# A hand-written TensorE order for the transform of a spectral layer: one pattern per step, the halves of the first stage set apart

## Chip, cores and metric

One core of one Trainium2 chip. The metric is device time in microseconds (us); the kernel before has a median of 1771.21 us over 3 runs (1770.46 to 1773.0).

## What is computed

`x` is (8, 3136, 256) in float32. The reference takes a real FFT over the sequence, multiplies by a complex 256x256 matrix, adds a complex bias, shrinks real and imaginary parts towards zero, transforms back, and feeds the result to a feed-forward block with a 3-tap convolution and a gate:

```python
X = np.fft.rfft(x, axis=1)
Yr = Xr @ w_r - Xi @ w_i + b_r
Yi = Xr @ w_i + Xi @ w_r + b_i
Y = sign(Y) * maximum(abs(Y) - 0.01, 0)          # both parts
y = np.fft.irfft(Y, n=3136, axis=1)
h = maximum(y @ w_in, 0)                          # 256 -> 1024
c = conv_w[0] * h[t-1] + conv_w[1] * h[t] + conv_w[2] * h[t+1]
out = (h * sigmoid(c)) @ w_out                    # 1024 -> 256
```

## The kernel before

3136 is 56 times 56, so each transform is two stages of products with small tables. The work of the transform is cut into 56 items, 7 for each of the 8 batches. It runs as a loop over steps (L373); step `it` touches several items at once:

- `load_a2` (L268) asks for the second-stage input of item it+2 from the DRAM scratch `sc1`.
- `stage2` (L273): eight float32 products of 128 columns on TensorE (PE), L280. ScalarE (ACT) and VectorE (DVE) split the result into a high part `fh` (L284, L287) and a low part `fl` (L286, L288), for products in three pieces.
- `load_inv1` and `load_t2`, in the first seven steps only: pieces of the tables of the inverse and the forward transform. Each piece of the inverse table lands in `i_raw`, which has two buffers; ACT casts it (L140, tile `i_hi`) and DVE takes the difference (L141, `i_lo`).
- `mix` (L291): the complex matrix on item it-1, as three groups of twelve products of 256 columns (L304), in three PSUM tiles `ps_mx`. DVE adds bias and combines (L309, L313), ACT and DVE shrink (L318, L319), ACT casts to `sh` (L320), GpSimd makes `sl`.
- `stage3` (L324): twelve products on item it-3 (L331), whose copy `z1` goes to the scratch `sc2`.
- `stage1` (L239): the first stage of an item some ten places ahead. Two float32 products of 512 columns (L245), called halves below. Both write the one buffer of the PSUM pool `ps1`, so a half can't begin before ACT has copied the half before it into `a1` (L246). `a1` has two buffers; each whole `a1` goes to `sc1` by a DMA (L247), so the third item after the head can't be copied before the first one's store has landed. The loaded `xr` has three buffers.

The first stage of the first batch's seven items stands before the loop (`stage1_head`, L249). Two more items, 7 and 8, are called ahead of the loop (L358 to L360). Item 7's two halves, item 8's and then item 9's are the first halves that this text speaks of.

The order of the instructions on each engine is not the written one: the program is built with a scheduler that orders every engine by its own estimate of times (`schedule_with_timeline_sim`, L537). All DMAs are issued on SyncE's queue (SP), in order. After the transform come `stage4` (L416) and the feed-forward loop (`up`, `down`, L432 to L484).

Of the kernel before, what the change touches and what calls it, by code (L numbers as in the profile page):

```python
# [9 lines left out]
F32 = mybir.dt.float32  # L10
# [4 lines left out]
ALU = mybir.AluOpType  # L15
# [3 lines left out]
B, S, D, FF = 8, 3136, 256, 1024  # L19
# [3 lines left out]
SP = 64  # L23
H = 28
LAM = 0.01
UG = 4
NG = U // UG
JC = 4
# [68 lines left out]
def spectral_ffn_kernel(ctx: ExitStack, tc: tile.TileContext, x, w_r, w_i, b_r, b_i,  # L97
                        w_in, conv_w, w_out, fwd1, fwd2, inv1, inv2, out):
    nc = tc.nc
    K1, K2 = 2 * R, 2 * SP  # L100

    dram = ctx.enter_context(tc.tile_pool(name="dram", bufs=1, space=DRAM))
    sc1 = [dram.tile([K1, H, D], F32, name=f"sc1_{b}") for b in range(B)]
# [13 lines left out]
    with ExitStack() as ab:  # L117
# [15 lines left out]
        bias = cmx.tile([P, 2, UG // 2, D], F32, name="bias")  # L133
# [60 lines left out]
        def split_weight(dst, raw, n, name):  # L194

            top, rest = yield from from_bits(raw, n, name)
            h, l = dst
            nc.scalar.copy(h, top)
            yield nc.vector.tensor_tensor(top, top, h.bitcast(F32), op=ALU.subtract)
            yield nc.vector.tensor_tensor(l, top, rest, op=ALU.add)  # L200
# [6 lines left out]
        def later():  # L207
            nc.sync.dma_start(i2, inv2)
            bits = [load_bits(conv_w[k].rearrange("(f p) w -> p f w", p=P), NF, "cw") for k in range(2)]
            for k in range(3):  # L210
                top, rest = yield from from_bits(bits[k], NF, "cw")
                yield nc.vector.tensor_tensor(cw[:, k, :], top, rest, op=ALU.add)  # L212
                if k == 0:
                    bits.append(load_bits(conv_w[2].rearrange("(f p) w -> p f w", p=P), NF, "cw"))
            pieces = []
            for t in range(NT):
                for c in range(0, FF, WP):
                    pieces.append(([q[:, t, c:c + WP] for q in win], winv[:, t, c:c + WP, :], "win"))
            for f in range(0, NF, 2):
                pieces.append(([q[:, f:f + 2, :].rearrange("p a d -> p (a d)") for q in wout], woutv[:, f:f + 2, :, :], "wout"))  # L220
            asked = []
            for n in range(len(pieces) + 1):
                if n < len(pieces):
                    dst, src, nm = pieces[n]
                    asked.append((dst, load_bits(src, WP, nm), WP, nm))
                    yield None
                if n:
                    yield from split_weight(*asked.pop(0))

        def load_x(pool, b, jc, parts=1, **kw):  # L230

            xr = pool.tile([K1, JC, D], F32, name="xr", **kw)
            xv = x[b].rearrange("(n j) d -> n j d", j=H)[:, jc * JC:(jc + 1) * JC, :]
            w = JC // parts
            for k in range(0, JC, w):
                ld = nc.sync.dma_start(xr[:, k:k + w, :], xv[:, k:k + w, :])
            return xr, ld

        def stage1(b, jc):  # L239

            xr, _ = load_x(s1p, b, jc, bufs=XRB)
            a1 = s1p.tile([K1, JC, D], F32, name="a1", bufs=2)
            for j in range(0, JC, 2):
                ps = ps1.tile([K1, 2, D], F32, name="ps_s1")
                nc.tensor.matmul(ps, f1, xr[:, j:j + 2, :], start=True, stop=True)  # L245
                nc.scalar.copy(a1[:, j:j + 2, :], ps)  # L246
            return nc.sync.dma_start(sc1[b][:, jc * JC:(jc + 1) * JC, :], a1)  # L247

        def stage1_head(xs, b=0):  # L249

# [17 lines left out]
        def load_a2(b, g):  # L268
            a2 = a2p.tile([K1, UG, D], F32, name="a2")
            ld = nc.sync.dma_start(a2, sc1[b].rearrange("(u q) j d -> (q j) u d", q=4)[:, g * UG:(g + 1) * UG, :])  # L270
            return a2, ld
# [16 lines left out]
            nc.vector.tensor_tensor(fl[:, :, 2], d, fh[:, :, 2].bitcast(F32), op=ALU.subtract)  # L288
            return fh, fl

        def mix(xs):  # L291


            fh, fl = xs
            ps = [psm.tile([K2, UG // 2, D], F32, name=f"ps_mx{c}") for c in range(3)]
            for c in (2, 0, 1):
                q = (1, 2, 0)[c]
                for k in range(UG // 2):
                    mm = []
                    for t in range(NT):  # L300
                        a = [f[:, t, c, 2 * k:2 * k + 2, :] for f in (fh, fl)]
                        mm += [(a[0], wmix_hi[:, t, q, :]), (a[0], wmix_lo[:, t, q, :]), (a[1], wmix_hi[:, t, q, :])]
                    for n, (lt, rh) in enumerate(mm):
                        nc.tensor.matmul(ps[c][:, k, :], lt, rh, start=(n == 0), stop=(n == len(mm) - 1))  # L304
            p1 = wk.tile([K2, 2, UG // 2, D], F32, name="p1", bufs=1)
            v = wk.tile([K2, UG // 2, 2, D], F32, name="v")
            half = (slice(0, SP), slice(SP, K2))
            for c in range(2):
                nc.vector.tensor_tensor(p1[:, c], ps[2], bias[:, c], op=ALU.add)  # L309
            for c in range(2):  # L310
                for k in range(2):
                    src, dst = half[k], half[k if c == 0 else 1 - k]
                    nc.vector.tensor_tensor(v[dst, :, k, :], ps[c][src], p1[src, c], op=ALU.add)  # L313
            v = v.rearrange("p a b d -> p (a b) d")
            sh = wk.tile([K2, UG, D], F32R, name="sh")
            sl = wk.tile([K2, UG, D], F32R, name="sl", bufs=1)
            r = wk.tile([K2, UG, D], F32, name="r", bufs=1)
            nc.scalar.activation(r, v, AF.Relu, bias=mlam)  # L318
            thr = nc.vector.scalar_tensor_tensor(v, v, LAM, r, op0=ALU.add, op1=ALU.min)  # L319
            nc.scalar.copy(sh, v)  # L320
            SL_ENG.tensor_tensor(sl, v, sh.bitcast(F32), op=ALU.subtract)  # L321
            return sh, sl, thr

        def stage3(b, g, s):  # L324

            sh, sl, _ = s
            ps = psa.tile([K1, UG, D], F32, name="ps_s3")
            for k in range(UG):
                u = g * UG + k
                for n, (lt, rh) in enumerate(((i1_hi, sh), (i1_hi, sl), (i1_lo, sh))):  # L330
                    nc.tensor.matmul(ps[:, k, :], lt[:, u, :], rh[:, k, :], start=(n == 0), stop=(n == 2))  # L331
            z1 = io.tile([K1, UG, D], F32, name="z1", bufs=2)
            nc.scalar.copy(z1, ps)
            nc.sync.dma_start(sc2[b][:, g * UG:(g + 1) * UG, :], z1)

        nc.vector.memset(mlam, -LAM)
        nc.vector.memset(warm, 0.0)
        nc.scalar.activation(warm, warm, AF.Sigmoid)

        AHEAD = NG + 3  # L340
        items = [(b, g) for b in range(B) for g in range(NG)]
        n_it = len(items)
        WP0, CW_IT = 3, 9
        a2s = {}
        p1 = NG
# [10 lines left out]
                st = stage1_head(xh)  # L356
        with tc.issue_after(st.ins):
            for _ in range(2):  # L358
                stage1(*items[p1])
                p1 += 1  # L360
            for i in range(2):
                a2s[i], ld = load_a2(*items[i])
        ab.enter_context(tc.issue_after(ld.ins))
        wkf, wk, cab, io = [ab.enter_context(tc.tile_pool(name=nm, bufs=n, reuse_waits="tile"))
                            for nm, n in (("wkf", 2), ("wk", 2), ("cab", 1), ("io", 2))]
# [3 lines left out]
        i1_hi = cab.tile([K2, U, K1], F32R, name="i1_hi")  # L369
        i1_lo = cab.tile([K2, U, K1], F32R, name="i1_lo")  # L370
        background = later()
        xs, ss = {}, {}
        for it in range(n_it + 3):  # L373
            if it + 2 < n_it:
                a2s[it + 2], _ = load_a2(*items[it + 2])
            if it < n_it:
                xs[it] = stage2(items[it][1], a2s.pop(it))
            if it < NG:
                load_inv1(it)
                if it + 1 < NG:  # L380
                    load_t2(it + 1)
            if 0 <= it - 1 < n_it:
                ss[it - 1] = mix(xs.pop(it - 1))
            if 0 <= it - 3 < n_it:
                stage3(*items[it - 3], ss.pop(it - 3))
            while p1 < n_it and p1 < min(it + AHEAD, NG + 2 + it + it // 2):
                stage1(*items[p1])
                p1 += 1
            if WP0 <= it < n_it:
                with tc.issue_after(ss[it - 1][2].ins):  # L390
                    for _ in range(5 if it < CW_IT else 2 + (it % 5 == 0)):
                        next(background, None)
# [6 lines left out]
    wk, hp, io, y_b = pool("cwk"), pool("chp", 3), pool("cio"), pool("y_b")  # L399
# [101 lines left out]
    for st in range(n_st + LAG):  # L501
        if st < n_st:
# [8 lines left out]
            if todo and f in (1, 4, 7):  # L511
                b, jg = todo.pop(0)
# [28 lines left out]
```

## Time and profile before

| | us |
|---|---|
| median of 3 runs | 1771.21 |
| the profiled execution, its own time | 1769.05 |
| span of the profiled execution | 1767.3 |
| PE busy / DVE busy / ACT busy | 1731.0 / 1524.3 / 1229.1 |
| the transform: last product of stage 3 (L331) starts | 561.49 |

Time in the profile is counted from the first instruction. A row of the timeline has the start, the length and, in square brackets, how long the engine sat idle before it and what it then waited for. PE's lengths include the drain of a product, so consecutive products overlap in the rows, and the cost of one is the distance from its start to the next start. A float32 product appears as two records (x2 for a half, x16 for the eight of stage 2). "SPq" rows are DMA issues; a DMA lands some us later.

### The profile page before, as it was taken

The numbers are of one execution on the slowest core, as the hardware profiler recorded it, in microseconds if no ns is written. First come the engines' busy times: TensorE is split into PE (matmuls) and PEld (weight loads), VectorE is DVE, ScalarE is ACT, GpSimd is POOL, SyncE is SP. The second block draws the span as 40 slices with busy tenths as digits, with TensorE's granted clock in tenths as the row PEclk, the third lists the DMA queues.
The fourth block names the chain that finished last, engine by engine and source line by source line (L and its number), as shares of the span: only waits on it lengthen the run. The fifth ranks groups of instructions, "written<-read, shape, count | busy, mean of one in ns | idle before, by whom it ended". The sixth has DMA issues, their size and how long they took to land.

```text
span 1767.3 us, 29387 instructions
## 1 busy us (share of the span) xinstructions
PE 1731.0 (98%) x12096; PEld 1621.6 (92%) x12096; DVE 1524.3 (86%) x1820; ACT 1229.1 (70%) x1590; POOL 134.7 (8%) x60
## 2 busy tenths in 40 slices
PE   6899999999998999999999999999999999999999
PEld 2788888888998999999999999999999999999998
DVE  2899999998896988988888888888888888888887
ACT  2667777776665777777777777777777777777766
POOL 0122222222232000000000000000000000000000
PEclk8999999999999999999999999999999999999999
DMA  9777677677534110111111011111101111100001
GB/s 263 216 230 236 196 232 216 192 230 228 164 111 136 43 43 22 32 53 53 32 53 53 22 55 51 49 46 52 43 22 43 53 43 43 42 22 22 22 22 42
DMA packets 107382, 164.63 MB, mean 93 GB/s; under 512 B 8816, under 2 KB 86000, under 8 KB 107248
## 3 DMA queue, kind: packets, MB, share of 16 engines
q1 hardware_dynamic: 107248, 162.74, 30.9%
q8 instruction: 96, 1.57, 0.4%
q14 instruction: 38, 0.31, 0.1%
HBM read 85.65 MB, written 77.07 MB: 92 GB/s over the span
## 4 chain that ended last, share of the span: by engine, by line
PE 93%; DMA 3%; DVE 1%; ACT 1%; issue 0%; SPq 0%; ACTq 0%
PE acc L470 31%; PE ps_h L442 31%; PE ps_mx L304 12%; PE ps_s L423 5%; PE ps_s L280 5%; PE ps_s L331 4%; PE ps_s L245 4%; DMA i_raw<-in_inv_dram 2%; DMA z<-sc 1%; DMA sc<-ha 0%; DMA a<-sc 0%; DMA sc<-a 0%; ACT a L246 0%; DVE cw L212 0%; DVE yl L430 0%
## 5 line engine op out<-in xcount | busy, mean ns | idle before, releaser
L470 PE MATMUL acc<-wout,gh 128*128 128x256 f32 x3136 | 567.0, 280 | 0.0
L451 DVE SCALAR_TENSOR_TENSOR c<-h,cw,c 128x896 f32<-128x896 f32 x448 | 513.1, 1147 | 47.3 <-ACT c L449 46.3
L442 PE MATMUL ps_h<-yh,win 128*128 128x450 f32 x1792 | 551.0, 368 | 0.1
L470 PEld LDWEIGHTS acc<-wout,gh 128*128 128x128 f32 x3136 | 493.7, 188 | 6.5
L470 PE MATMUL acc<-wout,gl 128*128 128x256 f32 x1568 | 437.6, 281 | 0.0
L444 ACT ACTIVATE h<-ps_h 128x900 f32<-128x900 f32 x224 | 207.7, 927 | 254.8 <-PE ps_h L442 254.8
L442 PEld LDWEIGHTS ps_h<-yh,win 128*128 128x128 f32 x1792 | 338.7, 189 | 26.4 <-DVE yl L430 0.8
L442 PE MATMUL ps_h<-yl,win 128*128 128x450 f32 x896 | 329.2, 367 | 0.0
L470 PEld LDWEIGHTS acc<-wout,gl 128*128 128x128 f32 x1568 | 293.7, 188 | 0.1
L457 DVE TENSOR_TENSOR gl<-c,gh 128x896 fp32r<-128x896 f32 x224 | 243.1, 1089 | 53.6 <-ACT gh L456 50.1
L453 DVE TENSOR_TENSOR c<-h,c 128x896 f32<-128x896 f32 x224 | 243.6, 1088 | 46.9 <-ACT c L452 46.7
L456 ACT CAST gh<-c 128x896 fp32r<-128x896 f32 x224 | 209.8, 942 | 49.4 <-DVE c L453 49.4
L452 ACT ACTIVATE c<-c 128x896 f32<-128x896 f32 x224 | 213.3, 952 | 23.9 <-DVE c L451 21.0
L304 PE MATMUL ps_mx<-wmix_lo,fh 128*128 128x256 f32 x672 | 202.2, 301 | 0.0
L304 PE MATMUL ps_mx<-wmix_hi,fh 128*128 128x256 f32 x672 | 196.9, 294 | 0.5 <-DVE v L313 0.3
L304 PE MATMUL ps_mx<-wmix_hi,fl 128*128 128x256 f32 x672 | 188.7, 282 | 1.3 <-DVE fl L288 1.2
L442 PEld LDWEIGHTS ps_h<-yl,win 128*128 128x128 f32 x896 | 168.9, 189 | 11.0
L449 ACT ACTIVATE c<-h,cw 128x896 f32<-128x896 f32 x168 | 175.5, 1044 | 2.6 <-DVE gl L457 0.2
L321 POOL TENSOR_TENSOR sl<-v,sh 128x1024 fp32r<-128x1024 f32 x56 | 134.5, 2402 | 423.1 <-PE ps_s L331 300.0
L313 DVE TENSOR_TENSOR v<-ps_mx,p 64x512 f32<-64x512 f32 x224 | 154.0, 688 | 3.3
L304 PEld LDWEIGHTS ps_mx<-wmix_lo,fh 128*128 128x128 f32 x672 | 126.4, 188 | 12.3 <-issue 12.3
L304 PEld LDWEIGHTS ps_mx<-wmix_hi,fl 128*128 128x128 f32 x672 | 126.0, 188 | 11.8 <-issue 9.9
(84 smaller groups left out, 2023.0 us busy)
## 6 DMA issues: line engine op xcount, KB each, us to landing
a<-sc SPq DMA_DIRECT2D x56, 448.0 KB, 5.0
sc<-z SPq DMA_DIRECT2D x56, 448.0 KB, 3.3
z<-sc SPq DMA_DIRECT2D x56, 448.0 KB, 3.8
xr<-in_x_dram SPq DMA_DIRECT2D x55, 448.0 KB, 4.7
out_dram<-o SPq DMA_DIRECT2D x27, 896.0 KB, 4.0
sc<-a SPq DMA_DIRECT2D x49, 448.0 KB, 4.9
sc<-ha SPq DMA_DIRECT2D x7, 448.0 KB, 7.5
win_bits<-in_moe_w_in_dram SPq DMA_DIRECT2D x4, 512.0 KB, 7.6
```

Source lines behind the costliest of these rows:

```text
L304: nc.tensor.matmul(ps[c][:, k, :], lt, rh, start=(n == 0), stop=(n == len(mm) - 1))
L313: nc.vector.tensor_tensor(v[dst, :, k, :], ps[c][src], p1[src, c], op=ALU.add)
L321: SL_ENG.tensor_tensor(sl, v, sh.bitcast(F32), op=ALU.subtract)
L442: nc.tensor.matmul(ps[:, a, 0:CH + 2], lt, rh, start=(n == 0), stop=(n == len(mm) - 1))
L444: nc.scalar.activation(h, ps[:, :, 0:CH + 2], AF.Relu)
L449: nc.scalar.mul(c, h[:, :, 0:CH], cw[:, 0, f:f + 1])
L451: nc.vector.scalar_tensor_tensor(c, h[:, :, k:k + CH], cw[:, k, f:f + 1], c, op0=ALU.mult, op1=ALU.add)
L452: nc.scalar.activation(c, c, AF.Sigmoid)
L453: nc.vector.tensor_tensor(c, h[:, :, 1:CH + 1], c, op=ALU.mult)
L456: nc.scalar.copy(gh, c)
L457: nc.vector.tensor_tensor(gl, c, gh.bitcast(F32), op=ALU.subtract)
L470: nc.tensor.matmul(acc[m // 2][:, m % 2, :], lt[:, sl], rh[:, f, :], start=(f == 0 and n == 0 and m % 2 == 0), stop=(f == NF - 1 and n == ...
```

## The change

PE's instructions in the transform are no longer ordered by the scheduler: a manual order for PE alone is opened ahead of the step loop, so PE gets the order in which the code is written. The other engines' instructions are still placed by the scheduler. To write the order, `stage1` and `mix` become generators that give up control after a product, and the loop draws from them.

```diff
-            return nc.sync.dma_start(sc1[b][:, jc * JC:(jc + 1) * JC, :], a1)
+                if j + 2 == JC:
+                    nc.sync.dma_start(sc1[b][:, jc * JC:(jc + 1) * JC, :], a1)
+                yield None
...
+        def some(g, n):
+            for _ in range(n):
+                next(g, None)
...
+        def halves(k):
+            for b, jc in firsts[k:]:
+                yield from stage1(b, jc)
+
+        first, given = halves(p1), 2 * p1
         xs, ss = {}, {}
+        ab.enter_context(tc.manual_schedule(engines={mybir.EngineType.PE}))
         for it in range(n_it + 3):
...
-            if 0 <= it - 1 < n_it:
-                ss[it - 1] = mix(xs.pop(it - 1))
+            due = 2 * p1 + 2 * (it + 1) + min(it, 2)
+            n_a, given = due - given, due
+            done = []
+            mx = mix(xs.pop(it - 1), done) if 0 <= it - 1 < n_it else iter(())
+            for i in range(n_a - 1):
+                some(mx, (10, 8, 8)[n_a - 2] if i == 0 else (0, 14, 10)[n_a - 2])
+                some(first, 1)
+            some(mx, 64)
+            ss[it - 1] = done[0] if done else None
             if 0 <= it - 3 < n_it:
                 stage3(*items[it - 3], ss.pop(it - 3))
-            while p1 < n_it and p1 < min(it + AHEAD, NG + 2 + it + it // 2):
-                stage1(*items[p1])
-                p1 += 1
+            some(first, 1)
```

From step 3 on, a step on PE is: stage 2; ten products of the mixing; a half; the other 26; stage 3; a half. Steps 1 and 2 have three halves (after 8, after 22 and at the end), step 0, which has no mixing, two. The first stage runs an item or a little more further ahead than before: 10 items after step 0 instead of 9, 14 after step 3 instead of 13.

Three places show what moves. The first is PE at the start of the loop. `ps_s_224` and `ps_s_227` are item 7's halves, `ps_s_234` and `ps_s_237` item 8's; products with `t_114` are stage 2, those with `wmix` the mixing. Before, from the second half of item 7:

```order
11 L245 MATMUL ps_s_227<-xr,f_113 112x512
12 L304 MATMUL ps_mx_322<-wmix_hi,fh 128x256
13 L304 MATMUL ps_mx_322<-wmix_lo,fh 128x256
14 L304 MATMUL ps_mx_323<-wmix_hi,fh 128x256
15 L304 MATMUL ps_mx_323<-wmix_lo,fh 128x256
16 L280 MATMUL ps_s_297<-t_114,a_243 128x128 x4
```

Now, from the same half (`ps_s_297` and `ps_s_300` are here item 9's halves):

```order
11 L245 MATMUL ps_s_227<-xr,f_113 112x512
12 L245 MATMUL ps_s_234<-xr,f_113 112x512
13 L245 MATMUL ps_s_237<-xr,f_113 112x512
14 L245 MATMUL ps_s_297<-xr,f_113 112x512
15 L245 MATMUL ps_s_300<-xr,f_113 112x512
16 L282 MATMUL ps_s_309<-t_114,a_243 128x128 x4
17 L282 MATMUL ps_s_318<-t_114,a_243 128x128 x4
18 L308 MATMUL ps_mx_336<-wmix_hi,fh 128x256
```

Five halves now stand back to back ahead of step 1's stage 2; before, one half of item 7 was followed by mixing at once, and the third item's halves came after step 2's stage 2.

The second place is ACT behind those halves: copies of halves (`a_...`) among the casts of the inverse table (`i_hi`) and the second stage's `d` and `fh`. Before, from the copy of item 8's first half; the row of `a_378` is item 9's first half, and the last row is the fourth of the seven casts:

```order
24 L246 COPY a_233<-ps_s_234 112x512
25 L283 COPY d<-ps_s_306 128x256
26 L284 CAST fh<-ps_s_306 128x512
27 L287 CAST fh<-d 128x2x256
28 L246 COPY a_233<-ps_s_237 112x512
29 L140 CAST i_hi<-i_raw 128x448
30 L283 COPY d<-ps_s_391 128x256
31 L284 CAST fh<-ps_s_391 128x512
32 L283 COPY d<-ps_s_400 128x256
33 L284 CAST fh<-ps_s_400 128x512
34 L246 COPY a_378<-ps_s_379 112x512
35 L140 CAST i_hi<-i_raw 128x448
```

Now, from the copy of item 9's first half (the third cast stands in the row ahead of it; the casts here are the fourth to the seventh, and `a_349` is item 10's first half):

```order
25 L246 COPY a_296<-ps_s_297 112x512
26 L140 CAST i_hi<-i_raw 128x448
27 L246 COPY a_296<-ps_s_300 112x512
28 L140 CAST i_hi<-i_raw 128x448
29 L285 COPY d<-ps_s_309 128x256
30 L286 CAST fh<-ps_s_309 128x512
31 L140 CAST i_hi<-i_raw 128x448
32 L285 COPY d<-ps_s_318 128x256
33 L286 CAST fh<-ps_s_318 128x512
34 L289 CAST fh<-d 128x2x256
35 L140 CAST i_hi<-i_raw 128x448
36 L246 COPY a_349<-ps_s_350 112x512
```

All seven casts now stand ahead of the copy of item 10's first half, and item 9's copies stand among them; before, step 2's second stage (`ps_s_391`, `ps_s_400`) stood ahead of the fourth cast.

The third place is SP's queue from the second-stage load of item 3 on: `a<-sc` loads, `i_raw` loads, `xr` loads, and stores `sc<-a`. Before:

```order
29 L270 DMA a_292<-sc_0_57 112x4x256
30 L168 DMA i_raw<-in_inv_dram 128x448
31 L236 DMA xr<-in_x_dram 112x1024
32 L247 DMA sc_1_58<-a_223 112x1024
33 L168 DMA i_raw<-in_inv_dram 128x448
34 L270 DMA a_386<-sc_0_57 112x4x256
35 L236 DMA xr<-in_x_dram 112x1024
36 L247 DMA sc_1_58<-a_233 112x1024
37 L270 DMA a_490<-sc_0_57 112x4x256
38 L168 DMA i_raw<-in_inv_dram 128x448 x2
```

Now:

```order
28 L272 DMA a_304<-sc_0_57 112x4x256
29 L168 DMA i_raw<-in_inv_dram 128x448
30 L236 DMA xr<-in_x_dram 112x1024
31 L248 DMA sc_1_58<-a_223 112x1024
32 L168 DMA i_raw<-in_inv_dram 128x448
33 L236 DMA xr<-in_x_dram 112x1024
34 L248 DMA sc_1_58<-a_233 112x1024
35 L168 DMA i_raw<-in_inv_dram 128x448 x2
36 L236 DMA xr<-in_x_dram 112x1024
37 L248 DMA sc_1_58<-a_296 112x1024
```

The third and fourth `i_raw` loads and the store of item 7 keep their places behind the same load; behind them the two second-stage loads of items 4 and 5 have moved back past the fifth and sixth `i_raw`. Further up, the load of item 9 moves ahead of the second `i_raw` load.

From the last product of the mixing to the end of the program all engines have the same rows in both kernels, but for the first products of stage 3 of the last items, one of which stands behind stage 4's first sixteen products now instead of ahead of them.

More of the change, by code (lines that the diff above doesn't have):

```diff
@@ L289, in stage2, with mix @@
             return fh, fl
-        def mix(xs):
+        def mix(xs, done):
             fh, fl = xs
             ps = [psm.tile([K2, UG // 2, D], F32, name=f"ps_mx{c}") for c in range(3)]
+            p1 = wk.tile([K2, 2, UG // 2, D], F32, name="p1", bufs=1)
+            v = wk.tile([K2, UG // 2, 2, D], F32, name="v")
+            half = (slice(0, SP), slice(SP, K2))
             for c in (2, 0, 1):
@@ L304, in mix @@
                         nc.tensor.matmul(ps[c][:, k, :], lt, rh, start=(n == 0), stop=(n == len(mm) - 1))
[L305 to L313, printed above, removed]
+                        if n < len(mm) - 1:
+                            yield None
+                    if k == 0:
+                        yield None
+                if c == 2:
+                    for i in range(2):
+                        nc.vector.tensor_tensor(p1[:, i], ps[2], bias[:, i], op=ALU.add)
+                else:
+                    for k in range(2):
+                        src, dst = half[k], half[k if c == 0 else 1 - k]
+                        nc.vector.tensor_tensor(v[dst, :, k, :], ps[c][src], p1[src, c], op=ALU.add)
+                if c != 1:
+                    yield None
             v = v.rearrange("p a b d -> p (a b) d")
@@ L321, in mix @@
             SL_ENG.tensor_tensor(sl, v, sh.bitcast(F32), op=ALU.subtract)
-            return sh, sl, thr
+            done.append((sh, sl, thr))
+            yield None
         def stage3(b, g, s):
-            sh, sl, _ = s
+            sh, sl = s[0:2]
             ps = psa.tile([K1, UG, D], F32, name="ps_s3")
@@ L338, in spectral_ffn_kernel @@
         nc.scalar.activation(warm, warm, AF.Sigmoid)
-        AHEAD = NG + 3
-        items = [(b, g) for b in range(B) for g in range(NG)]
+        items = firsts = [(b, g) for b in range(B) for g in range(NG)]
         n_it = len(items)
@@ L358, in spectral_ffn_kernel @@
             for _ in range(2):
-                stage1(*items[p1])
+                some(stage1(*firsts[p1]), 2)
                 p1 += 1
@@ L381, in spectral_ffn_kernel @@
                     load_t2(it + 1)
-            if 0 <= it - 1 < n_it:
-                ss[it - 1] = mix(xs.pop(it - 1))
+            due = 2 * p1 + 2 * (it + 1) + min(it, 2)
[7 more added lines that the diff above has]
+            ss[it - 1] = done[0] if done else None
             if 0 <= it - 3 < n_it:
                 stage3(*items[it - 3], ss.pop(it - 3))
-            while p1 < n_it and p1 < min(it + AHEAD, NG + 2 + it + it // 2):
-                stage1(*items[p1])
-                p1 += 1
+            some(first, 1)
             if WP0 <= it < n_it:
```

## Prediction

> **What bounds it now.** I read PE first, since the page gives it 1731.0 of 1767.3 us: the stages by windows, to see where it isn't full. Columns: the stretch, its length, PE's busy time (records), then the other engines, the granted clock, the DMA share.
>
> ```profile
> 0.00:45.00 45.00, 27.54 (x70) 13.24 (x71) 11.88 (x21) 11.38 (x21) 0.20 (x4) 0.85 0.95 262
> 45.00:90.00 45.00, 40.10 (x288) 34.59 (x287) 37.94 (x63) 27.92 (x50) 7.16 (x3) 1.00 0.79 216
> 90.00:135.00 45.00, 42.59 (x306) 36.65 (x304) 42.24 (x77) 30.40 (x51) 12.23 (x5) 1.00 0.80 236
> 135.00:180.00 45.00, 45.00 (x336) 40.05 (x336) 43.58 (x72) 32.52 (x51) 11.37 (x6) 1.00 0.72 228
> ```
>
> From 135 us on PE is full; the loop's losses lie between 39 and 135 us. Next, what PE waited for from 36 to 135 us (sum, times, longest):
>
> ```profile
> PE ps_s L245 <- ACT a L246: 6.0, 5, 2.2
> PE ps_s L280 <- DMA a<-sc: 2.4, 2, 1.3
> PE ps_mx L304 <- DVE v L313: 0.3, 1, 0.3
> PE ps_s L280 <- DMA t<-in_fwd_dram: 0.3, 1, 0.3
> ```
>
> 9.0 us in nine waits, most of it halves whose buffer ACT had not emptied. Then a full step on PE's timeline, for whether "full" hides waits, and for prices by the distance between starts:
>
> ```profile
> 302.15 0.28 PE L304 MATMUL ps_mx<-wmix_hi,fh 128*128 128x256 f32 x1
> 302.27 0.28 PE L304 MATMUL ps_mx<-wmix_lo,fh 128*128 128x256 f32 x1
> ...
> 306.02 1.02 PE L245 MATMUL ps_s<-xr,f 112*112 112x512 f32 x2
> 306.88 1.95 PE L280 MATMUL ps_s<-t,a 112*128 112x128 f32 x16
> 308.58 0.37 PE L304 MATMUL ps_mx<-wmix_hi,fh 128*128 128x256 f32 x1
> ```
>
> A 256-column product costs 0.12, a half 0.86, a second stage 1.70. A step is 48 products at 0.117, two halves and a second stage: 5.6 + 1.7 + 1.7 = 9.0 us. 45 us hold five such steps of 68 records each, 340, and the row shows 336 begun: there is next to nothing to gain after 135 us, in whatever order the products stand. What the change can move is the idle time before that.
>
> **Why ACT was late.** ACT's rows in the same stretch, the table casts (L140) and two copies of halves (L246):
>
> ```profile
> 42.76 0.57 ACT L140 CAST i_hi<-i_raw 128x448 fp32r<-128x448 f32 x1 [0.53 <-DMA i_raw<-in_inv_dram]
> 43.23 0.58 ACT L246 COPY a<-ps_s 112x512 f32<-112x512 f32 x1
> 53.75 0.57 ACT L140 CAST i_hi<-i_raw 128x448 fp32r<-128x448 f32 x1 [4.30 <-DMA i_raw<-in_inv_dram]
> 56.29 0.59 ACT L246 COPY a<-ps_s 112x512 f32<-112x512 f32 x1 [0.45 <-DMA sc<-a]
> 57.16 0.56 ACT L140 CAST i_hi<-i_raw 128x448 fp32r<-128x448 f32 x1 [0.29 <-DMA i_raw<-in_inv_dram]
> 64.64 0.57 ACT L140 CAST i_hi<-i_raw 128x448 fp32r<-128x448 f32 x1 [2.31 <-DMA i_raw<-in_inv_dram]
> 71.73 0.56 ACT L140 CAST i_hi<-i_raw 128x448 fp32r<-128x448 f32 x1 [3.00 <-DMA i_raw<-in_inv_dram]
> 72.20 0.58 ACT L246 COPY a<-ps_s 112x512 f32<-112x512 f32 x1
> ```
>
> These are casts 2, 3, 4, 5 and 7: ACT sits in front of them until a load lands, and whatever stands behind waits too. The row at 56.29 is item 9's first copy, held by the store of item 7 (two `a1` buffers). The last row is a half's copy released only by cast 7; PE's longest wait (2.2) is the half behind it. The issues, on SP:
>
> ```profile
> 48.16 0.43 SPq L168 DMA_DIRECT2D i_raw<-in_inv_dram  x1
> ...
> 49.16 0.38 SPq L247 DMA_DIRECT2D sc<-a  x1
> 49.63 0.38 SPq L168 DMA_DIRECT2D i_raw<-in_inv_dram  x1
> ...
> 55.01 4.29 SPq L168 DMA_DIRECT2D i_raw<-in_inv_dram  x2
> ...
> 65.89 0.35 SPq L168 DMA_DIRECT2D i_raw<-in_inv_dram  x1
> ```
>
> Loads 3 and 4, then 5 and 6, then 7: two buffers, so load 5 waits for cast 3 and its subtraction, load 7 for cast 5.
>
> **The change, part by part.** What the edit gives: the early waits of before go. Without the first of the nine (1.33 at 35.97, ahead of the loop's rows that change) 7.7 us are left; each wait costs about 0.16 more than its bracket, since the product before it drains meanwhile:
>
> ```profile
> 54.94 0.27 PE L304 MATMUL ps_mx<-wmix_hi,fl 128*128 128x256 f32 x1
> 56.93 1.11 PE L245 MATMUL ps_s<-xr,f 112*112 112x512 f32 x2 [1.72 <-ACT a L246]
> ```
>
> Start to start 1.99, less 0.12 is 1.87 for a bracket of 1.72. Eight times 0.16 is 1.3; two slow starts near 41 us add about 1. Together before loses about 10 us from 39.55 on, and I take all of it as gone.
>
> What it costs, first stretch. PE must now pass five halves before anything else:
>
> ```profile
> 32.62 2.02 PE L245 MATMUL ps_s<-xr,f 112*112 112x512 f32 x2 [10.57 <-DMA xr<-in_x_dram]
> 35.97 3.79 PE L280 MATMUL ps_s<-t,a 112*128 112x128 f32 x16 [1.33 <-DMA a<-sc]
> 39.55 1.56 PE L245 MATMUL ps_s<-xr,f 112*112 112x512 f32 x2
> 40.47 0.75 PE L304 MATMUL ps_mx<-wmix_hi,fh 128*128 128x256 f32 x1
> ```
>
> Everything up to the half at 39.55 is as before. Behind it stand item 8's two halves and item 9's first, each waiting for the copy of the one before. That chain reaches item 9's first half by about 48 us (copies of 0.59 between halves of 0.86, cast 2 among them). Its copy stands behind cast 3 (53.75) and behind the landing of item 7's store (56.29); both transfers stand in SP's queue behind the same work as before, so I take their times over. The copy ends at 56.9, and item 9's second half begins at 57.0. From 39.55 to 57.0 are 17.45 us; PE does four halves in them, 3.4 us, and 0.5 more for the slow start that before has too. Lost: 13.5 us. The second stage of step 1 and all mixing stand behind on PE and can't fill the hole; before, that is what PE did there. If load and store landed faster than any row here (5.6 and 3.1 us after issue, below) ACT would be free at about 54.3: 11.5 lost.
>
> ```profile
> DMA to landing us min/median/max: 5.6/7.5/9.6
> ...
> DMA to landing us min/median/max: 3.1/7.0/9.8
> ```
>
> The first row is the seven table loads, the second five stores of first-stage items.
>
> Second stretch. From 57.0 PE has item 9's second half, step 1's second stage, eight products, a half of item 10, fourteen products: 0.86 + 1.70 + 0.94 + 0.86 + 1.64 = 6.0 us. Then comes item 10's second half, which needs the copy of the first, and that copy stands behind casts 4 to 7. Load 5 is issued at 55.01 again; with 5.6 to 9.6 us to landing, cast 5 is at 60.6 to 64.6. Before, load 7 went out 1.25 us behind cast 5 (64.64 to 65.89) and cast 7 followed 5.84 later. So cast 7 comes at 67.5 to 71.7. I take 68.0, near the lower end, because two second-stage loads of 448 KB that shared the DMA engines ahead of load 5 have moved back. Cast, copy and hand-over (0.5 + 0.6 + 0.1) let PE go on at 69.2. Of 12.2 us it works 6.0: 6.2 lost (5.7 to 9.9).
>
> Slow clock. The half at 32.62 came after 10.57 us of idle and took 2.02, not 1.02; the second stage at 35.97 took 3.79, not 1.95. Short waits can do it too, as after the transform:
>
> ```profile
> 548.73 0.37 PE L331 MATMUL ps_s<-sh,i_hi 128*112 128x256 f32 x1 [2.12 <-ACT sh L320]
> 548.94 5.35 PE L423 MATMUL ps_s<-i,z 112*128 112x112 f32 x32
> ...
> 563.90 4.05 PE L423 MATMUL ps_s<-i,z 112*128 112x112 f32 x32 [0.36 <-DMA z<-sc]
> ```
>
> After 2.12 us of idle, 32 records took 5.35 instead of 4.05. So a slow spell costs 1.3 us (these rows) to about 3.4 (1.0 + 1.84 + 0.5 at 32.62, 35.97 and 39.55). The one behind the first hole is paid by the second, which ends with cast 7 anyway. Behind the second hole (4.2 us idle or less) I take 2.3; none is possible.
>
> The Trainium skill, TensorE: Matmul & The Clock Gate, section "What's actually happening", says the clock is halved after at least one idle window of about 3.4 us and restored after one busy one; by that the spell would cost at least half of 3.4, an estimate of 1.7, and the sum would be 0.6 lower. The halving after 10.57 us agrees, that after 2.12 doesn't quite, so the rows decide.
>
> Beyond that nothing waits. A step's halves lie 2.9 us (second stage, ten products) and 4.4 us (38 products) apart, against a copy of 0.59 behind at most one other ACT row; item 13, last of batch 1, is done at step 3 and needed at step 7, where before had a 1.1 us wait. DVE has 43.58 of 45 us in the window above: it follows PE, and each of its results is used a step later at the earliest. The reordered products of stage 3 near the end cost nothing: the sixteen behind them wait for DVE either way.
>
> Sum: 13.5 + 6.2 + 2.3 - 10 = +12.0 us. The profiled execution (1769.05, span 1767.3) is 2.2 below the median; I add the difference to the median: 1771.2 + 12.0 = **1783.2**.
>
> **Rivals.** *The early waits go and nothing takes their place* (faster): if casts and stores were in time, 10 us come off: 1761.2. It decides by cast 3 and the store coming by 44 us, when item 8 is done; but load 3 is issued at 48.16 only. 0.06. *Only the first hole* (no change): 11.5 lost, no second, 10 gained: 1772.7. For that cast 7 must come by 63, against 67.5 at the earliest by the rows. 0.08. *Loads as slow as before*: cast 7 at 71.7 costs 3.7 more, the spell 3.4: 1788.0. Likely if the `xr` loads moved up take the freed bandwidth. 0.14. *DVE becomes the bound*: 1.4 us of slack in 45 us is 0.3 a step; if its new order idles 0.6 a step, it costs 0.3 in each; thirty such steps lose 9 us more: 1792. Against it, its idle time is waiting for PE's side. 0.04. The forecast has 0.68. That the order isn't what was written is excluded by the listing.
>
> **Numbers.** About 0.2%, 3.5 us, is what a measurement here can tell from no change. Slower: 0.68 + 0.14 + 0.04 = 0.86; same 0.08; faster 0.06. Low end: 11.5 + 5.7 + 0 - 10 = 7.2, and a little of the no-change case, 1775. High end 1788.0 and a little of the DVE case, 1789.
>
> **What would show it.** Right: PE idle from about 48 to 57 us with item 9's copy starting near 56.3; again until about 69 behind cast 7; a slow spell after; the transform's last product some 12 us later than 561.49; full windows from 95 us on. Wrong: item 9's second half before 54; a copy of item 10 ahead of cast 7's landing; waits at the halves after 135 us; DVE idle growing in the windows from 135 us on.

## The result, and the profile after

The changed kernel takes 1814.07 us (median of 4 runs, 1811.63 to 1821.63), against 1771.3 for the kernel before in the same session: a ratio of 1.0247, 95% interval 1.0215 to 1.0280. It is slower, by 43 us where 12 were forecast. The profiled execution took 1812.48 us, its span is 1810.7. The last product of the transform's stage 3 starts at 604.8 us, 43.3 later than before, so the whole loss lies in the transform.

The windows first, in longer stretches than the prediction's. Before:

```profile
0.00:135.00 135.00, 110.23 (x659) 84.48 (x659) 92.06 (x159) 69.70 (x122) 19.59 (x12) 0.95 0.85 238
135.00:360.00 225.00, 225.00 (x1678) 200.73 (x1678) 213.47 (x347) 162.97 (x259) 57.21 (x25) 1.00 0.72 215
360.00:495.00 135.00, 135.00 (x1027) 122.11 (x1026) 120.46 (x191) 92.12 (x149) 36.45 (x16) 1.00 0.68 199
```

After:

```profile
0.00:135.00 135.00, 102.23 (x574) 76.07 (x575) 79.29 (x138) 62.25 (x109) 14.41 (x10) 0.87 0.78 224
135.00:360.00 225.00, 212.84 (x1520) 184.68 (x1519) 219.87 (x318) 146.81 (x236) 54.82 (x23) 0.99 0.67 199
360.00:495.00 135.00, 135.00 (x1007) 120.38 (x1006) 122.12 (x196) 93.36 (x152) 33.47 (x16) 1.00 0.70 208
```

Read PE's record counts, not its busy share: 1678 records filled 225 us before, 7.46 a us, and 158 fewer are done in the same stretch now. That is 21.2 us lost between 135 and 360 us, where the prediction had none. Up to 135 us 85 records are missing; each weighed by the prediction's prices they are 9.6 us of work. From 360 to 495 us PE is full again. What is left of the span's 43.4 us, 12.6, is a remainder; it goes after that, in the last rounds of the transform, in which no halves are left. DVE's column shows the odd thing: it does less work in the middle (318 instructions, not 347) and is busy longer (219.87, not 213.47).

What PE waited for from 135 to 360 us, after (sum, times, longest):

```profile
PE ps_mx L308 <- DVE fl L290: 8.8, 14, 1.3
PE ps_s L245 <- ACT a L246: 2.7, 7, 1.2
```

Before has no wait in this stretch. The first row is the mixing's third product, which needs the third `fl` of its item. DVE's groups there, after:

```profile
L319 DVE TENSOR_TENSOR v<-ps_mx,p 64x512 f32<-64x512 f32 x92 | 63.2, 687 | 1.3
L290 DVE TENSOR_TENSOR fl<-d,fh 128x512 fp32r<-128x512 f32 x23 | 32.2, 1399 | 0.0
L288 DVE TENSOR_TENSOR fl<-ps_s,fh 128x512 fp32r<-128x512 f32 x44 | 29.9, 679 | 0.0
```

and the same operation before:

```profile
L288 DVE TENSOR_TENSOR fl<-d,fh 128x512 fp32r<-128x512 f32 x24 | 17.1, 712 | 0.0
```

One shape, one engine: the `fl` that is read out of PSUM takes 679 ns, the `fl` whose two inputs lie in SBUF takes 1399, and 712 in the kernel before. (None of the 44 read out of PSUM begins while GpSimd works here; experiment 2 has some that do.) A step in which it shows, after, DVE and then GpSimd (POOL):

```profile
257.93 1.89 DVE L290 TENSOR_TENSOR fl<-d,fh 128x512 fp32r<-128x512 f32 x1
259.74 2.80 DVE L319 TENSOR_TENSOR v<-ps_mx,p 64x512 f32<-64x512 f32 x4
```

```profile
256.91 2.36 POOL L329 TENSOR_TENSOR sl<-v,sh 128x1024 fp32r<-128x1024 f32 x1 [8.01 <-ACT fh L289]
```

and such a step of the kernel before:

```profile
250.15 0.69 DVE L288 TENSOR_TENSOR fl<-d,fh 128x512 fp32r<-128x512 f32 x1
250.75 2.81 DVE L313 TENSOR_TENSOR v<-ps_mx,p 64x512 f32<-64x512 f32 x4
```

```profile
251.43 2.37 POOL L321 TENSOR_TENSOR sl<-v,sh 128x1024 fp32r<-128x1024 f32 x1 [6.61 <-PE ps_s L331]
```

GpSimd's subtraction waits for stage 3 and lasts 2.36 us either way. (The bracket after names an ACT row that ended at the same moment; stage 3's last product starts at 256.57 and lasts 0.28.) Before, the third `fl` starts 1.28 us ahead of the subtraction and is done 0.59 ahead of it (250.84 against 251.43), and the subtraction lies beside the four `v`, which read PSUM and lose nothing: 2.81. After, the `fl` comes 1.02 us behind the subtraction's start, stands until it ends at 259.27 and finishes 0.55 later. Not every step is like this one: in most of the others a background conversion is held in its place, as one of 512 columns at 247.46, 1.72 us for 0.42. A held instruction counts as busy, which is why DVE looks busier.

Now the start of the program, where the prediction put its holes. PE's halves after:

```profile
41.80 1.69 PE L245 MATMUL ps_s<-xr,f 112*112 112x512 f32 x2 [2.08 <-ACT a L246]
44.52 2.05 PE L245 MATMUL ps_s<-xr,f 112*112 112x512 f32 x2 [1.03 <-ACT a L246]
56.35 2.05 PE L245 MATMUL ps_s<-xr,f 112*112 112x512 f32 x2 [7.06 <-ACT a L246]
58.19 3.62 PE L282 MATMUL ps_s<-t,a 112*128 112x128 f32 x16
67.20 1.11 PE L245 MATMUL ps_s<-xr,f 112*112 112x512 f32 x2 [1.51 <-ACT a L246]
```

ACT's copies that release the third and the last of them:

```profile
55.71 0.58 ACT L246 COPY a<-ps_s 112x512 f32<-112x512 f32 x1 [1.75 <-DMA sc<-a]
66.10 0.56 ACT L140 CAST i_hi<-i_raw 128x448 fp32r<-128x448 f32 x1 [2.28 <-DMA i_raw<-in_inv_dram]
66.57 0.58 ACT L246 COPY a<-ps_s 112x512 f32<-112x512 f32 x1
```

Both holes are there, with the causes named: item 9's copy behind the store of item 7, item 10's behind the seventh cast. The halves at 44.52 and 56.35 and the second stage at 58.19 run at half speed (2.05 for 1.02, 3.62 for 1.95); the granted clock is 0.80 from 45 to 90 us, where it was 1.00 before.

### The profile page after: what moved, and what is told of

The parts are those of the page before. It is cut to its first block, busy times and chain, and to the rows that moved or that the text cites. A ratio compares the mean times of both kernels' runs of the same rounds, so it can differ in the third digit from the quotient of the medians.

```text
span 1810.7 us, 29392 instructions
## 1 busy us (share of the span) xinstructions
PE 1744.7 (96%) x12096; PEld 1627.8 (90%) x12096; DVE 1557.4 (86%) x1820; ACT 1228.5 (68%) x1590; POOL 133.1 (7%) x60
## 4 chain that ended last, share of the span: by engine, by line
PE 81%; DVE 10%; issue 3%; DMA 3%; ACT 2%; SPq 0%; DVEq 0%; ACTq 0%
PE acc L493 31%; PE ps_h L465 30%; PE ps_mx L308 8%; PE ps_s L446 5%; DVE v L319 3%; PE ps_s L245 3%; PE ps_s L340 3%; PE ps_s L282 2%; DVE fl L290 2%; DVE fl L288 1%; DMA i_raw<-in_inv_dram 1%; DVE p L315 1%; DVE v L327 1%; DVE d L287 1%; ACT r L326 1%
## 5 line engine op out<-in xcount | busy, mean ns | idle before, releaser
L308 PE MATMUL ps_mx<-wmix_hi,fl 128*128 128x256 f32 x672 | 193.5, 288 | 23.0 <-DVE fl L290 21.2
L308 PE MATMUL ps_mx<-wmix_lo,fh 128*128 128x256 f32 x672 | 207.7, 309 | 0.0
```

## The experiments

The theory, "port": while GpSimd's subtraction runs, a DVE instruction out of SBUF alone stands still; that makes the third `fl` late, PE waits for it, stage 3 and with it the next subtraction move along, and so on. The rival, "order": DVE is late by its new order, and GpSimd has no part.

**1. GpSimd's subtraction left out, in the changed kernel and, as a control, in the kernel before.** Both leave a part of the computation out: the low part of stage 3's operand.

```diff
-            sl = wk.tile([K2, UG, D], F32R, name="sl", bufs=1)
+            sl = sh
...
-            SL_ENG.tensor_tensor(sl, v, sh.bitcast(F32), op=ALU.subtract)
```

> The changed kernel without GpSimd's subtraction (stage 3 multiplies sh a second time in place of sl, so PE does the same number of products and the output is not the reference's). Theory P (port): VectorE instructions that read and write only SBUF stand still while GpSimd's subtraction runs, and in the changed kernel fl<-d,fh falls into it, so PE waits for VectorE. Then without GpSimd the waits of the mixing for fl go, the windows from 135 us are full and only the early holes are left: 1776 to 1785 us. Theory O (order): the new order makes VectorE late by itself, fl stands behind p. Then GpSimd plays no part: 1808 to 1816 us.

Measured: 1788.69 us (1786.96 to 1792.19), ratio to the kernel before 1.0113 (1.0094 to 1.0132). PE waits for nothing from 135 to 360 us, and the third `fl` has its old length:

```profile
L290 DVE TENSOR_TENSOR fl<-d,fh 128x512 fp32r<-128x512 f32 x24 | 16.4, 682 | 0.0
```

The waits for `fl` that remain, over the whole execution (sum, times, longest), all nine behind 440 us:

```profile
PE ps_mx L308 <- DVE fl L290: 7.6, 9, 2.5
```

> The kernel before without GpSimd's subtraction (sh in place of sl, as in the run beside it), as a control for what leaving it out is worth by itself. Theory P: the subtraction lies beside v<-ps_mx,p, which reads PSUM and is not slowed, so 1768 to 1772 us. Theory O: the same. If this one gains as much as the changed kernel does, leaving the work out is worth that anyway and the pair says nothing.

Measured: 1769.31 us, ratio 0.9996 (0.9982 to 1.0009). So the subtraction costs the kernel before nothing and the changed one some 24 us (1.0247 against 1.0113). "Order" falls for the middle. The result is 4 us above port's range, though: something else is lost at the end, where PE waits 7.6 us for `fl` with no subtraction beside it.

**2. The subtraction in four pieces, and, in the kernel before, done twice.**

```diff
+            for k in range(0, UG, UG // 4):
+                q = slice(k, k + UG // 4)
+                SL_ENG.tensor_tensor(sl[:, q, :], v[:, q, :], sh[:, q, :].bitcast(F32), op=ALU.subtract)
```

> The changed kernel with GpSimd's subtraction of 1024 columns cut into four of 256. Theory P: a VectorE instruction that meets it waits for the rest of a quarter (about 0.6 us) and not for the rest of the whole (up to 2.4 us), if it gets in between; fl<-d,fh comes down from a mean of 1.4 us towards 0.9 and the time to 1780 to 1800 us. Theory O: no change, 1808 to 1816 us.

Measured: 1793.22 us (1790.47 to 1795.03), ratio 1.0133 (1.0113 to 1.0153): 20 us less than the changed kernel by the ratios, with the same work on every engine, for which GpSimd even takes longer (741 ns a piece on average). The middle is full, the third `fl` 683 ns.

> The kernel before with GpSimd's subtraction done twice in a row (the second writes the same sl; 4.8 us of GpSimd in a step of 9.1 us, and PE needs sl some 5 us after it begins). Theory P: the second run lies beside the shrinking and the conversion of weights, which read SBUF; VectorE loses 0.7 to 1.2 us a step, more than its slack of about 0.5, and PE waits: 1785 to 1815 us, with longer means of fl<-d,fh or v<-v,r. Theory O: GpSimd has time to spare, 1769 to 1774 us.

Measured: 1836.54 us (1832.31 to 1841.77), ratio 1.0383 (1.0358 to 1.0407), well above the range of either theory: port's direction, and more than its size. The old order falls into the same loss when GpSimd works long enough to reach the third `fl`, for which alone PE waits from 135 to 360 us (18.3 us):

```profile
L288 DVE TENSOR_TENSOR fl<-d,fh 128x512 fp32r<-128x512 f32 x21 | 39.1, 1862 | 0.0
L286 DVE TENSOR_TENSOR fl<-ps_s,fh 128x512 fp32r<-128x512 f32 x43 | 29.2, 680 | 0.0
```

The second row is the control: 8 of these 43 `fl`, which are read out of PSUM, begin while GpSimd works, and each takes 0.68 us.

**3. Place or length.** First, in the changed kernel, the round's last half ahead of stage 3 instead of behind it, which moves the subtraction about 0.86 us later and leaves its length:

```diff
+            some(first, 1)
             if 0 <= it - 3 < n_it:
                 stage3(*items[it - 3], ss.pop(it - 3))
-            some(first, 1)
```

> The changed kernel with the round's last first half ahead of stage 3 in place of behind it: GpSimd's subtraction, which waits for stage 3, then starts about 0.86 us later in the step, beside the four v of VectorE rather than beside the third fl; its length and VectorE's order stay. Theory place (what costs is that a VectorE operation out of SBUF begins while GpSimd's subtraction runs, 1.0 us after its start in the changed kernel): most of the middle's 21 us goes, 1790 to 1800 us, the fl<-d,fh group of 135 to 360 us under 0.9 us a piece. Rival length (whatever the place, 2.38 us of GpSimd beside VectorE cost the same): 1809 to 1817 us and fl<-d,fh over 1.2 us.

Measured: 1790.58 us (1789.25 to 1793.01), ratio 1.0123 (1.0103 to 1.0143); the third `fl` is at 683 ns with the subtraction whole:

```profile
L290 DVE TENSOR_TENSOR fl<-d,fh 128x512 fp32r<-128x512 f32 x24 | 16.4, 683 | 0.0
```

Both early holes are still there (PE waits 12.3 us for the halves between 36 and 135 us, 12.4 in the changed kernel). So the place decides. Next, `sl` with two buffers, the subtraction 0.8 us earlier:

> The changed kernel with two buffers for sl, so GpSimd's subtraction no longer waits for stage 3 and starts as soon as ScalarE's sh is there, at 256.1 in place of 256.9 us in the step looked at; it would end at 258.5, and the third fl, which begins at 257.9, would be held for 0.5 us and not for 1.2. Theory place: part of the 21 us goes, 1793 to 1807 us. Rival length: 1809 to 1817 us.

Measured: 1813.96 us (1812.95 to 1819.93), ratio 1.0261 (1.0236 to 1.0285): the rival's number. One step of it, DVE and GpSimd:

```profile
254.46 1.17 DVE L290 TENSOR_TENSOR fl<-d,fh 128x512 fp32r<-128x512 f32 x1
```

```profile
252.70 2.38 POOL L329 TENSOR_TENSOR sl<-v,sh 128x1024 fp32r<-128x1024 f32 x1 [7.28 <-ACT sh L328]
```

The `fl` is held 0.5 us, as I had reckoned, and yet nothing is won: the subtraction now follows DVE's own chain (`v`, then ACT's `sh`, its releaser in the row), so it is as late as DVE is and the two never come apart. The loss is smaller in a step and goes on past 360 us. Then two pieces in place of four:

> The changed kernel with GpSimd's subtraction in two pieces of about 1.2 us in place of one of 2.38 or four of 0.7. Theory: an operation of VectorE that comes while a piece runs is held until that piece ends, so half of 1.2 us on average and at most 1.2; the middle loses under half of its 21 us, 1793 to 1803 us. Rival (not the length of a piece but GpSimd's whole time decides, and four pieces helped by chance of phase): 1809 to 1817 us.

Measured: 1815.08 us (1811.89 to 1818.89), ratio 1.0261 (1.0233 to 1.0289); again no gain, and inside the rival's range. Its trace:

```profile
255.28 1.56 DVE L290 TENSOR_TENSOR fl<-d,fh 128x512 fp32r<-128x512 f32 x1
```

```profile
253.78 2.51 POOL L331 TENSOR_TENSOR sl<-v,sh 128x512 fp32r<-128x512 f32 x2 [7.21 <-PE ps_s L342]
```

The `fl` waits for the second piece only, 0.88 us more than its 0.68; "half a piece on average" was a wrong reckoning. My reading, which no run tests: DVE is not struck at random, it falls back until the hold is as large as what PE gives way. That four pieces helped by chance of phase, as the rival had it, is unlikely: the middle is free of PE waits in all four programs in which the changed kernel has them (two are below, one at the end of section 5). Last, the pieces in the kernel before:

> The kernel before with the subtraction in four pieces. Theory: there it already lies beside VectorE's readers of PSUM, which it does not hold up, so the pieces are worth nothing: ratio 0.998 to 1.002, 1766 to 1774 us. Rival (pieces help wherever GpSimd works): 1755 to 1765 us.

Measured: 1771.61 us (10 runs), ratio 1.0013 (1.0002 to 1.0024): nothing won, as expected.

**4. The holes and the last rounds.** Later first halves (`a_late`), which leave item 10's copy no row of casts to stand behind and so take the second hole away:

```diff
-            due = 2 * p1 + 2 * (it + 1) + min(it, 2)
+            due = 2 * p1 + (0, 2, 5)[it] if it < 3 else 2 * p1 + 2 * it + 2
...
-            some(first, 1)
+            if n_a:
+                some(first, 1)
```

> The changed kernel with its first halves asked for later: none in the first round, two in the second, three in the third, then two a round (in place of three, three, two). It undoes only the clump of casts ahead of the copies of items 9 and 10. Theory sum (three losses, each by itself: two holes at the start about 9.6 us, GpSimd holding VectorE up from 110 to 332 us about 21 us, the last part without halves about 12 us): the holes shrink by 6 to 9.6 us and the middle stays as it was, 1803 to 1809 us, the fl<-d,fh group of 135 to 360 us still over 1.1 us a piece. Rival chain (the holes at the start are what makes VectorE late enough to meet GpSimd; without them it never does): the middle is full as well, 45.00 us of PE in each window from 90 to 450 us, 1780 to 1788 us.

Measured: 1805.2, 1805.7, 1821.0 and 1822.3 us, ratio 1.0248 (1.0198 to 1.0298). The spread says little; the trace of the shortest execution does. One hole is gone and the first is 5.1 us long in place of 7.1, and the middle is lost all the same:

```profile
L290 DVE TENSOR_TENSOR fl<-d,fh 128x512 fp32r<-128x512 f32 x23 | 30.0, 1305 | 0.0
```

`a_swap` is the other half of the argument, both holes and a full middle. So the holes don't decide it. With the pieces as well:

> The later first halves and GpSimd's subtraction in four pieces, both in the changed kernel. Theory sum: the holes (6 to 9.6 us) and GpSimd's part (about 21 us) go, the last part stays: 1783 to 1788 us, with nine waits of PE for fl between 480 and 560 us as in the run with four pieces alone. Rival chain: with the pieces the middle was free already, and the later halves add nothing or move the loss elsewhere: 1791 to 1796 us.

Measured: 1779.15 us (1777.36 to 1781.57), ratio 1.0057 (1.0038 to 1.0075), against 1.0133 with the pieces alone: the first halves are worth some 13 us. That is below the range of both theories (1783 to 1788, 1791 to 1796). The last rounds, PE handed back to the scheduler from round 46 on:

```diff
+            if it == 46:
+                ms.close()
```

> The changed kernel with PE's order handed back to the scheduler from round 46 on, when no halves are left; all before it as in the changed kernel. Theory sum: in those last rounds VectorE's order is what costs (the third fl of a block stands behind all four v), so 7 to 12 us go: 1802 to 1807 us, with no waits of PE for fl after 500 us. Rival (the last part is late only because GpSimd's subtraction lies beside it there too): the order does not matter, 1811 to 1817 us.

Measured: 1810.27 us (1806.58 to 1828.13), ratio 1.0250 (1.0198 to 1.0301): not told apart from the changed kernel, and between the two ranges expected. In its windows the stretch from 495 us is full, though:

```profile
495.00:540.00 45.00, 45.00 (x381) 44.06 (x379) 43.08 (x67) 29.50 (x45) 14.30 (x6) 1.00 0.44 131
```

In the changed kernel:

```profile
495.00:540.00 45.00, 40.69 (x340) 39.42 (x338) 43.06 (x62) 28.66 (x43) 13.79 (x6) 1.00 0.40 117
```

41 more records are 5 us. But this execution had done 40 records fewer by 135 us already (534 for 574), long before the edit acts, and that cancels the gain. All three edits together:

> All three edits together: later first halves, four pieces, and the scheduler's own order of PE from round 46 on. Theory sum: what the three take away adds up, 1770 to 1777 us, level with the kernel before or up to 0.4% above it. Rival (they share one cause and overlap): 1780 us or more.

Measured: 1774.5 us (10 runs, 1770.15 to 1777.55), ratio 1.0030 (1.0020 to 1.0041). That is 4.7 us below the run without the last edit, with intervals that just touch, and the nearest to the kernel before of all that were tried; none is faster. In the changed kernel's last rounds DVE's order puts the third `fl` behind all four `v`, right into the subtraction (529.04 to 531.41), and PE waits about a us for it in each round:

```profile
527.47 2.79 DVE L319 TENSOR_TENSOR v<-ps_mx,p 64x512 f32<-64x512 f32 x4
530.29 1.67 DVE L290 TENSOR_TENSOR fl<-d,fh 128x512 fp32r<-128x512 f32 x1
```

```profile
532.01 0.38 PE L308 MATMUL ps_mx<-wmix_hi,fl 128*128 128x256 f32 x1 [1.00 <-DVE fl L290]
```

The kernel before has it ahead of them:

```profile
524.89 0.69 DVE L288 TENSOR_TENSOR fl<-d,fh 128x512 fp32r<-128x512 f32 x1
525.49 2.81 DVE L313 TENSOR_TENSOR v<-ps_mx,p 64x512 f32<-64x512 f32 x4
```

These nine waits are 10.8 us. Without any subtraction (experiment 1) 7.6 were left, so here DVE's order seems to be the larger part and the hold the smaller.

**5. Why the kernel before escapes.** Between 135 and 360 us both kernels have nearly one pattern on PE: ten products of the mixing, a half, the other 26 and twelve of stage 3, a half, a second stage. So I looked for the meeting that starts the loss. After, DVE and GpSimd:

```profile
106.07 2.31 DVE L186 TENSOR_SCALAR cw_e<-cw_e 128x8 int32<-128x8 int32 x1
115.57 2.47 DVE L290 TENSOR_TENSOR fl<-d,fh 128x512 fp32r<-128x512 f32 x1
```

```profile
105.99 2.36 POOL L329 TENSOR_TENSOR sl<-v,sh 128x1024 fp32r<-128x1024 f32 x1 [6.76 <-PE ps_s L340]
115.13 2.36 POOL L329 TENSOR_TENSOR sl<-v,sh 128x1024 fp32r<-128x1024 f32 x1 [6.78 <-PE ps_s L340]
```

A background conversion of 8 columns (0.16 us elsewhere) comes 0.08 us behind the subtraction and is held 2.15; a step later the third `fl` begins 0.44 behind the subtraction, for which it had been 1.2 to 1.4 ahead in the three steps before. (At 76.94 us one had been held for 0.44 and the next was ahead again.) With four pieces the same conversion was held 0.5:

```profile
109.74 0.65 DVE L186 TENSOR_SCALAR cw_e<-cw_e 128x8 int32<-128x8 int32 x1
```

Last, two edits of the conversions: none in rounds 9 to 12, or fewer in every round.

```diff
-                    for _ in range(5 if it < CW_IT else 2 + (it % 5 == 0)):
+                    for _ in range(5 if it < CW_IT else (2 + (it % 5 == 0)) * (it > 12)):     # a_gap
+                    for _ in range(5 if it < CW_IT else 1 + it % 2):                          # a_relax
```

> The changed kernel without VectorE's background conversions in rounds 9 to 12 (they follow later; about two per round, 0.17 to 0.69 us each). The trace of the changed kernel shows the first held operation of that kind at 106.07 us (2.31 us for an 8-column conversion), and from the next step on the third fl is held. Theory start (one held operation tips VectorE from one steady state into the other, in which it meets GpSimd each step): without it the middle stays full, 45.00 us of PE in each window from 135 to 360 us, 1790 to 1797 us. Rival recur (the order brings VectorE beside GpSimd again whenever it has some 2 us of conversions to do): the loss only begins later, 1803 to 1817 us.

Measured: 1795.68 us (1794.33 to 1797.20), ratio 1.0147 (1.0130 to 1.0164). The time lies in the range of theory "start", but by luck: I had the gap in the wrong place. The held conversion still comes (at 107.98), and some 2 us are lost behind 135 us (323 records, not 337). Up to 155 us the conversions are the changed kernel's, about 2 us later; from there to 190 there are none. Both runs have one long step, 12.5 us between two subtractions, in which DVE catches up (to 157.98 in the changed kernel, to 159.82 here). The changed kernel, with one conversion more in it (0.68 us at 156.64), starts its `fl` only 0.14 ahead and is held again in the next step; this one is 0.74 ahead, and stays ahead when the conversions come back:

```profile
135.00:180.00 45.00, 43.41 (x323) 38.54 (x323) 42.25 (x66) 29.85 (x47) 12.00 (x5) 1.00 0.73 222
180.00:225.00 45.00, 45.00 (x336) 40.05 (x335) 42.49 (x70) 32.98 (x56) 12.07 (x5) 1.00 0.67 214
225.00:270.00 45.00, 45.00 (x337) 40.05 (x336) 42.35 (x69) 31.88 (x52) 11.95 (x5) 1.00 0.69 213
```

From 190 us on this is the changed kernel's order again, with its conversions at their old rate and the subtraction whole, and it loses nothing. So one program has two steady states in the middle, and the time depends on which one it enters. In the full one of the kernel before the third `fl` starts 0.4 to 1.7 us ahead of the subtraction from 135 to 360 us. Once it comes behind (307.88 against 306.24), is held 0.6, and is ahead again a step later, with no wait of PE: one meeting alone need not tip a kernel over.

> The changed kernel with 1.5 background conversions a round on average from round 9 on, in place of 2.2, so VectorE has about 0.4 us a step more to spare until they are used up (later than in the changed kernel). Theory start: the held operation still comes, but VectorE catches up sooner, 1793 to 1808 us. Rival recur with the place alone deciding: 1809 to 1817 us.

Measured: 1805.6, 1831.2, 1832.9 and 1836.0 us; the ratio of the two shorter ones is 1.0275 (1.0190 to 1.0361). The only trace is that of the longest. In it more spare time does not bring DVE out: it has 3 of 45 us free, and PE still loses:

```profile
225.00:270.00 45.00, 43.38 (x313) 37.62 (x312) 41.97 (x62) 30.51 (x50) 11.01 (x5) 1.00 0.60 186
```

The shortest, 1805.6, lies in theory "start"'s range, so whether spare time helps in some executions stays open.

> GpSimd's subtraction whole, with the three other edits: later first halves, the scheduler's order of PE from round 46 on, 1.5 conversions a round. If VectorE's spare time decides, 1774 to 1790 us; if the place of the whole subtraction decides whatever the spare time, 1795 to 1808 us.

Measured: 1785.4, 1786.0, 1807.8 and 1816.0 us; the ratio of the three shorter ones is 1.0132 (1.0066 to 1.0198). One program gives times of both theories' ranges; only the execution of 1807.8 has a trace, and its middle is lost. That the two short ones stayed in the full state is likely, not shown.

> The same with the subtraction in four pieces, so the run with all three edits plus 1.5 conversions a round: 1768 to 1777 us, since the middle was full already and spare time on VectorE buys nothing there.

Measured: 1776.96 us (1774.78 to 1778.71), ratio 1.0039 (1.0026 to 1.0052): with pieces, spare time on DVE buys nothing, as expected.

## Why the prediction was wrong, point by point

**The early losses** (13.5, 6.2 and 2.3, less 10, net 12.0). Right in mechanism and nearly in size: PE resumes at 56.35 (57.0 forecast) and 67.20 (69.2), and is 9.6 us behind at 135. The second hole was too dear, a wait of 1.51 us and not about 4, because its load came sooner and because PE reached it later: the slow clock lies ahead of it, not behind, where the prediction had put its 2.3 us (the half at 67.20 takes 1.11). PE runs at half speed until 62.5 us; the stretch behind the first hole alone, 56.35 to 62.5, costs 3.1 us. That the sum comes out near 12 is in part luck: one term was too large, one in the wrong place. The Trainium skill, TensorE: Matmul & The Clock Gate, "What's actually happening", asks for an idle window of about 3.4 us before the clock halves; here a wait of 2.08 us was enough, behind which the half at 41.80 (1.69 for 1.02) slows in its course.

**"There is next to nothing to gain after 135 us, in whatever order"** is true, and it hid the question that mattered: what there was to lose. The third `fl` starting 0.4 to 1.7 us ahead of the subtraction was the whole margin.

**"Beyond that nothing waits", and of DVE, "it follows PE, each of its results is used a step later at the earliest"**: this is the step that failed. The third `fl` is used a step later, but that means about 3 us later (ready at 250.84, first wanted about 254 before); and DVE's instructions had no fixed length in these runs. Beside GpSimd the third `fl` took 1.2 to 2.9 us in place of 0.68. It cost 21 us by the records, and by the experiments 20 (ratio 1.0247 to 1.0133). The trace of before had the warning, a conversion of 8 columns held for the length of a subtraction, and ahead of it an `fl` that came first and made the subtraction the longer one (2.73):

```profile
91.62 0.68 DVE L288 TENSOR_TENSOR fl<-d,fh 128x512 fp32r<-128x512 f32 x1
92.22 2.33 DVE L212 TENSOR_TENSOR cw<-cw_m,cw_rest 128x8 f32<-128x8 f32 x1
```

```profile
91.79 2.73 POOL L321 TENSOR_TENSOR sl<-v,sh 128x1024 fp32r<-128x1024 f32 x1 [8.00 <-PE ps_s L331]
```

There PE was still waiting for other things (42.59 of 45 us), and DVE was ahead again by 122.31 (the subtraction follows at 123.49); that the one let the other happen is likely, not shown. The Trainium skill, SBUF — State Buffer, "Who interferes with whom", has the rule: a VectorE instruction with two inputs in SBUF and a GpSimd instruction that reads SBUF exclude each other, and the second to come waits for the whole of the first; one with at most one SBUF input doesn't contend, outside the modes that use two ports, which `tensor_scalar` is listed as able to enter. The rows agree: the `fl` out of SBUF is held (1399 ns), the 8 out of PSUM that begin beside GpSimd in the kernel with the subtraction twice are not (0.68 us each), and the conversion at 106.07, a TENSOR_SCALAR with one input, is held too. No trace shows in which mode that one ran. I never asked who else was running beside DVE.

**"The reordered products of stage 3 near the end cost nothing"**: I looked at two products and not at the rounds without halves. There a step is 5.6 + 1.7 = 7.3 us on PE, DVE had no time to spare already before (the row below), and its order changed with PE's. The term was put at nothing, and lost are 12.6 us, the remainder of the span; giving PE back to the scheduler returns some 5 (1.0057 to 1.0030, intervals that touch).

```profile
495.00:540.00 45.00, 44.53 (x383) 44.13 (x381) 44.48 (x76) 31.25 (x48) 14.32 (x6) 1.00 0.31 93
```

**The rival "DVE becomes the bound"** (0.04) named the engine and priced idling of 0.3 us a step. It wasn't idling; the price was 21.2 us over some 23 steps, 0.9 each. Its sign to look for, idle time growing on DVE, would have missed it: idle time shrank, since a held instruction shows as a long one.

**What stays open.** That it is the single conversion at 106 us which tips the changed kernel wasn't tried by itself, nor what brings it back near 338 us. That the first halves are worth some 13 us with pieces, where the records give 9.6, is partly explained by the two profiled executions, whose spans are 15.8 us apart: by the records weighed as above 9.5 of these are there at 135 us, nothing is added up to 540, and from 540 to 620 the granted clock is 0.89 with the pieces alone and 0.98 with later halves, which is 7 us of 80 by an estimate from these two numbers. Why the clock differs there isn't known.

## What to carry to other kernels

Before a full engine is called safe, measure by how much its nearest input is early, and list which other engines' long instructions lie beside the one that makes it: a lead of 0.4 to 1.7 us in a 9 us step was lost behind one held instruction of 8 columns, and the loss then kept itself up for 200 us. Look at an instruction's mean length by shape in both traces, not only at idle time. If GpSimd and VectorE must share a step, put GpSimd's work beside VectorE's readers of PSUM, or cut it into short pieces: four were short enough here, two were not.

## What the hardware showed that I had not expected

A VectorE instruction of 128 x 8 elements took 2.31 us in place of 0.16 beside a GpSimd subtraction of 2.36, and 0.65 beside one in pieces of 0.7. The hold goes the other way too: behind an `fl` that came first the subtraction took 2.73 us. The same program held two steady states, 45.00 and about 42.6 us of PE in 45, and passed from one to the other in mid-run: before 360 us in the changed kernel, before 180 us in the run with the gap.
